# Cluster attention and two MLPs: tokens compared with centroids by small matmuls instead of wide ones and transposes back

## The chip, the core and the metric

The kernel runs on one core of a Trainium2 chip. The metric is the device time of one execution in microseconds. A core has engines that run side by side and wait for each other by semaphores: PE (TensorE) multiplies matrices and writes to PSUM, DVE (VectorE) and ACT (ScalarE) work elementwise and empty PSUM, POOL (GpSimd) works elementwise on SBUF, SP issues DMAs. In the profile PE stands for matmuls and PEld for the loads of their stationary operand.

## What is computed

Attention with a mask made from clusters, then two MLPs (reference, cut to what matters):

```python
q_n = q / (norm(q) + 1e-06); k_n = k / (norm(k) + 1e-06); c_n = centroids / (norm(centroids) + 1e-06)
q_assign = argmax(einsum('bhsd,hcd->bhsc', q_n, c_n), axis=-1)
k_assign = argmax(einsum('bhsd,hcd->bhsc', k_n, c_n), axis=-1)
mask = q_assign[:, :, :, None] == k_assign[:, :, None, :]
scores = where(mask, matmul(q, k.transpose(0, 1, 3, 2)) / sqrt(D), -1e9)
attn = softmax(scores)
x = matmul(attn, v)                       # batch 2, heads 8, tokens 768, width 64; 16 centroids per head
x = (sigmoid(x @ w_gate) * (x @ w_val)) @ w_out
out = relu(x @ w_in2)**2 @ w_out2         # the weights are float64 and are decoded on the chip
```

## The kernel before

All matmuls work on float32 numbers split into a high part of type float32r and a rest (`hi`, `lo`), so that a product takes several matmuls. Two heads of one batch make a pair; there are 8 pairs. Attention runs in 96 units, 12 per pair (2 heads, 2 halves, 3 blocks of 128 queries). In unit n the loop at L926 does, in this order: the maximum of unit n's scores on DVE (L935); what earlier groups left to do on ACT and DVE (`drain`); the transposes on PE of the probabilities of unit n-3 (`evac`, L821) and their copies by ACT (L823) and DVE (L829); the scores of unit n+1 on PE (`scores`, L803); the exponential on ACT (L956); four matmuls with the values of an earlier half (`attend`, L839, L840); and then the steps of the next pair's preparation that a table assigns to this unit. POOL normalises the probabilities (L875).

The preparation of a pair (`prep`) turns q and k (`transposes`, L563; after that hi and lo lie with the head width on the partitions and the tokens along the free dimension), compares the tokens with the 16 centroids of each head, takes the argmax (L656), builds a one-hot row per token (L663 to L679), transposes it (L696) and writes it beside q and k as the mask. The comparison takes four steps per pair: `sims(0)` and `sims(1)` ("s0", "s1") for three blocks of 128 tokens each, and `back(0)` and `back(1)` ("b0", "b1"). `cen` holds the centroids, high and low part, for both heads, with zeros around them.

The tables `STEPS` and, for the second pair, `SECOND_STEPS` say in which unit each step stands, counted from the first unit of the pair that is prepared. The first pair's preparation runs ahead of the loop as a plain list, and between its steps `keep_warm` puts transposes of the identity on PE (L888, the table `WARM`).

What a step computes in PSUM goes into a tile "t" of a pool with three buffers (`ps_t`), which `evac` uses too. Its evacuation (`post`) stands in the next unit's `drain`.

Of the kernel before, what the change touches and what calls it, by code (L numbers as in the profile page):

```python
# [8 lines left out]
F32 = mybir.dt.float32  # L9
# [19 lines left out]
STEPS = {  # L29
    -8: ["tq0"],  # L30
    -7: ["tk0"],
    -6: ["s0"],
    -5: ["tk1"],
    -4: ["tq1"],
    -3: ["b0", "load"],
    -2: ["s1"],
    -1: ["kb", "b1"],
    0: ["qb", "am"],
    1: ["eq"],
    2: ["oh", "on", "ka", "qa"],  # L40
# [5 lines left out]
    -3: ["tk0"],  # L46
    -2: ["tq0"],
    -1: ["tk1"],
    0: ["s0", "tq1"],
    1: ["s1"],  # L50
    2: ["b0", "kb"],
    3: ["b1", "qb"],
    5: ["am"],
    6: ["eq"],
    7: ["oh", "on", "ka", "qa"],
    9: ["mk"],
}

WARM = {-9: 8, -2: 16, -1: 4}


EARLY_PARTS = [3, 3, 9, 10, 15, 18, 19, 21, 27, 30, 30, 33, 34, 39, 42, 43, 45, 51]
# [10 lines left out]
def cluster_attention_two_mlps(  # L73
# [13 lines left out]
    nc = tc.nc  # L87
    B, H, S, D = q.shape
    NCL = centroids.shape[1]
    P = 128  # L90
# [5 lines left out]
    HB = NB // 2  # L96
    NH = HB * P
# [44 lines left out]
    for c in range(CH, F1 // P, CH):  # L142
        a = weights.index(("g", c + CH // 2))
# [175 lines left out]
    with tc.manual_schedule():  # L319
        ident = const.tile([P, P], F32, name="ident")  # L320
# [18 lines left out]
        cen = const.tile([P, 4 * NPAIR + 2, 2 * NCL], F32R, name="cen")  # L339
# [14 lines left out]
        act, parts, banks, split, sgs = {}, {}, {}, {}, {}  # L354
# [99 lines left out]
        with ExitStack() as ac:  # L454
# [3 lines left out]
            am = pc.enter_context(tc.tile_pool(name="am", bufs=1, side="right"))  # L458
# [5 lines left out]
            ps_t = ac.enter_context(tc.tile_pool(name="ps_t", bufs=3, space=PSUM))  # L464
# [83 lines left out]
            def prep(i):  # L548

                b, hp = pairs[i]  # L550
                hi_t, lo_t, keep = {}, {}, {}
# [58 lines left out]
                def sims(n):  # L610


                    def go():
                        sp = ps_t.tile([P, NH], F32, name="t")
                        parts = [(nm, t) for nm in "kq" for t in (hi_t, lo_t)]
                        for x, (nm, t) in enumerate(parts):
                            w = cen[:, 4 * hp + 2 : 4 * hp + 6] if nm == "k" else cen[:, 4 * hp : 4 * hp + 4]
                            nc.tensor.matmul(  # L618
                                sp, w.rearrange("p a c -> p (a c)"), t[nm][:, n * NH : (n + 1) * NH], start=(x == 0), stop=(x == 3)
                            )  # L620

                        def post():
                            keep["sim", n] = am.tile([P, NH], F32, name="sim", bufs=2)
                            nc.scalar.copy(keep["sim", n], sp)

                        return post

                    return go

                def back(n):  # L630
                    def go():
                        bp = ps_t.tile([P, HB, 2, 2, 2 * NCL], F32, name="t")
                        sim = keep.pop(("sim", n))
                        for c in range(HB):
                            nc.tensor.transpose(
                                bp[:, c].rearrange("p a b c -> p (a b c)"), sim[:, c * P : (c + 1) * P], ident
                            )

                        def post():
                            if n == 0:  # L640
                                keep["tot"] = am.tile([P, NB, 2, 2 * NCL], F32, name="tot")
                            o = keep["tot"][:, n * HB : (n + 1) * HB]
                            part = am.tile([P, HB, 2, 2 * NCL], F32, name="part")
                            nc.scalar.copy(part, bp[:, :, :, 1])
                            nc.vector.tensor_tensor(out=o, in0=bp[:, :, :, 0], in1=part, op=ALU.add)

                        return post

                    return go
# [84 lines left out]
                if i == 0:  # L734
                    return [
                        transposes("k", 0),
                        transposes("k", 1),
                        transposes("q", 0),
                        transposes("q", 1),
                        sims(0),  # L740
                        sims(1),
                        stack("k", 0),
                        stack("q", 0),
                        stack("q", 1),
                        back(0),
                        back(1),
                        argmax,
                        equal,
                        stack("k", 1),
                        onehot,  # L750
                        one,
                        first_mask,
                    ]
# [5 lines left out]
                    "load": lambda: load(i + 1, "kq"),  # L759
                    "s0": sims(0),  # L760
                    "s1": sims(1),
                    "b0": back(0),
                    "b1": back(1),
                    "ka": stack("k", 0),
                    "kb": stack("k", 1),
                    "qa": stack("q", 0),
# [137 lines left out]
            for t, f in enumerate(prep0):  # L904
# [9 lines left out]

                keep_warm(WARM.get(t - len(prep0), 0))
            outs, late, st = {}, {}, {}
# [4 lines left out]
            for i in range(1, len(pairs)):  # L921
                for m, group in (prep1 if i == 1 else prep(i)).items():
                    at = (i - 1) * UPP + m
                    todo.setdefault(at, []).append(group)
            st[0] = scores(units[0])
            for n in range(N + LAG + 4):  # L926
                u = units[n] if n < N else None
                w = units[n - LAG] if 0 <= n - LAG < N else None
# [7 lines left out]
                nm = nms.pop(n - 1, None)  # L936
                if nm is not None:
                    p = Pt[units[n - 1]]
# [32 lines left out]
                if w is not None:  # L971
                    Pt.pop(w)
                    if w[3] == HB - 1:
# [3 lines left out]
                        if w[1] == 1:  # L977
                            for t in range(3):
                                at = n + SUMS[w[2]][t] if w[0] < len(pairs) - 1 else n + (3 if end else 6)
# [65 lines left out]
```

## Time and profile before

| | |
|---|---|
| time, median of 3 runs | 820.93 us (820.81 to 821.15) |
| the profiled execution | 821.03 us, its span 819.2 us |
| PE, share of the span with a matmul in it | 98% |
| PEld / DVE / ACT / POOL | 84% / 76% / 54% / 26% |
| start until the first unit's maximum | 0 to 19.8 us |
| attention | to about 266 us |
| the two MLPs | about 266 to 819 us |

The median is over three executions. The profile is of one more, and every duration below is from that one. A busy share counts the time in which at least one instruction of the engine is on record; matmuls overlap in it, so that of PE says little by itself. The chain that ended last is followed back from the last instruction, at each step to what released it.

### The profile page before, as it was taken

What the parts mean: (1) busy time and instruction counts of PE and PEld (TensorE: products, weight loads), DVE (VectorE), ACT (ScalarE), POOL (GpSimd) and SP (SyncE); (2) the same over time, 40 slices, a digit from 0 to 9 for tenths busy, and PEclk for the clock granted to TensorE, in tenths of its full rate; (3) what the DMA queues carried; (4) which work ended last, traced back from release to release, by engine and by line L of the source; (5) the groups of instructions that cost most, each with busy time, mean ns of one, the idle gap of its engine ahead of it and who ended that gap; (6) DMA issues with size and microseconds to landing.
All of it is one profiled execution on the core that took longest, in us unless ns stands there. A gap on an engine that the chain in (4) does not pass through costs nothing.

```text
span 819.2 us, 11691 instructions
## 1 busy us (share of the span) xinstructions
PE 803.1 (98%) x4097; PEld 689.8 (84%) x4097; DVE 625.9 (76%) x1144; ACT 442.1 (54%) x889; POOL 214.2 (26%) x349
## 2 busy tenths in 40 slices
PE   7899999999999999999999999999999999999998
PEld 6789989999998788888888888888888888888886
DVE  5899999999898378657878767769784787788233
ACT  5888889888896223532332223336745733642530
POOL 4668989988884200000000000000000000000000
PEclk9999999999999999999999999999999999999999
DMA  8465455364321122122221212202222212221012
GB/s 190 108 144 144 102 136 121 92 143 96 78 77 44 52 71 95 51 71 68 94 77 52 78 52 78 78 0 89 66 78 77 78 52 77 78 78 52 0 52 102
DMA packets 63274, 67.01 MB, mean 82 GB/s; under 512 B 28624, under 2 KB 54224, under 8 KB 63216
## 3 DMA queue, kind: packets, MB, share of 16 engines
q1 hardware_dynamic: 63216, 66.27, 29.3%
q8 instruction: 32, 0.52, 0.3%
q14 instruction: 26, 0.21, 0.1%
HBM read 45.12 MB, written 3.15 MB: 59 GB/s over the span
## 4 chain that ended last, share of the span: by engine, by line
PE 80%; DVE 12%; POOL 3%; ACT 2%; issue 1%; DMA 1%; SPq 0%; POOLq 0%; ACTq 0%; DVEq 0%
PE bank_b L427 18%; PE bank_a L350 13%; PE bank_a L351 13%; PE bank_a L349 13%; PE bank_a L427 9%; DVE pt_lo L829 4%; PE t L821 4%; DVE nm L935 3%; PE s L803 3%; PE o L839 2%; PE o L840 2%; POOL p L875 1%; PE t L618 1%; PE t L563 1%; PE o L888 1%
## 5 line engine op out<-in xcount | busy, mean ns | idle before, releaser
L350 PE MATMUL bank_a<-x_lo,w 128*128 128x512 f32 x480 | 187.0, 389 | 0.9 <-POOL x_lo L870 0.9
L349 PE MATMUL bank_a<-x_hi,w 128*128 128x512 f32 x480 | 186.9, 389 | 0.0
L351 PE MATMUL bank_a<-x_hi,w 128*128 128x512 f32 x480 | 186.9, 389 | 0.0
L393 DVE TENSOR_TENSOR slo<-act,shi 128x512 fp32r<-128x512 f32 x84 | 57.9, 689 | 66.8 <-ACT shi L392 60.3
L350 PEld LDWEIGHTS bank_a<-x_lo,w 128*128 128x128 f32 x480 | 90.1, 188 | 19.7 <-POOL x_lo L870 1.2
L349 PEld LDWEIGHTS bank_a<-x_hi,w 128*128 128x128 f32 x480 | 90.1, 188 | 18.8 <-POOL x_hi L868 0.2
L351 PEld LDWEIGHTS bank_a<-x_hi,w 128*128 128x128 f32 x480 | 90.1, 188 | 18.8
L829 DVE TENSOR_TENSOR pt_lo<-t,pt_hi 128x384 fp32r<-128x384 f32 x192 | 96.7, 546 | 5.4 <-ACT pt_hi L823 5.4
L875 POOL TENSOR_SCALAR p<-p,nm,ones 128x768 f32<-128x768 f32 x96 | 94.8, 988 | 15.7 <-DVE nm L874 15.3
L956 ACT ACTIVATE p<-s,nm 128x768 f32<-128x768 f32 x96 | 88.0, 917 | 15.9 <-DVE nm L874 10.8
L803 PE MATMUL s<-st_k,st_q 128*128 128x384 f32 (+1 forms) x384 | 91.0, 359 | 0.6 <-ACT p L956 0.5
L935 DVE TENSOR_REDUCE nm<-s 128x1 f32<-128x768 f32 x96 | 91.0, 948 | 0.0
L823 ACT CAST pt_hi<-t 128x384 fp32r<-128x384 f32 x192 | 83.2, 487 | 6.3 <-PE t L821 5.6
L821 PE MATMUL t<-ident,p 128*128 128x128 f32 x576 | 81.6, 275 | 4.3 <-DVE pt_lo L829 3.2
L392 ACT CAST shi<-act 128x512 fp32r<-128x512 f32 x84 | 51.7, 615 | 56.0 <-PE bank_b L427 32.9
L427 PE MATMUL bank_b<-wo,shi 128*128 128x512 f32 x256 | 78.8, 389 | 0.0
L231 ACT CAST w<-wtop 128x512 fp32r<-128x512 f32 x38 | 23.7, 623 | 101.8 <-DVE wtop L249 101.8
L821 PEld LDWEIGHTS t<-ident,p 128*128 128x128 f32 x576 | 66.2, 140 | 11.7 <-issue 4.2
L839 PE MATMUL o<-pt_hi,vt 128*128 128x384 f32 x192 | 65.1, 339 | 0.4 <-ACT oc L845 0.4
L375 DVE TENSOR_TENSOR act<-bank_a,sg 128x512 f32<-128x512 f32 x36 | 24.9, 691 | 53.1 <-PE bank_a L351 50.9
L803 PEld LDWEIGHTS s<-st_k,st_q 128*128 128x128 f32 (+1 forms) x384 | 62.5, 190 | 2.9 <-ACT p L956 2.2
L840 PE MATMUL o<-pt_lo,vt 128*128 128x384 f32 x192 | 64.7, 337 | 0.0
(137 smaller groups left out, 1386.2 us busy)
## 6 DMA issues: line engine op xcount, KB each, us to landing
wraw<-in_moe_w_out_dram SPq DMA_DIRECT2D x28, 512.0 KB, 3.2
wraw<-in_moe_w_in_dram SPq DMA_DIRECT2D x16, 512.0 KB, 3.7
wraw<-in_moe_w_gate_dram SPq DMA_DIRECT2D x11, 512.0 KB, 3.5
wraw<-in_moe_w_val_dram SPq DMA_DIRECT2D x11, 512.0 KB, 3.5
nat_v<-in_v_dram SPq DMA_DIRECT2D x8, 384.0 KB, 3.2
st_k<-st_k SPq DMA_DIRECT2D x16, 192.0 KB, 4.5
x<-oc SPq DMA_DIRECT2D x32, 96.0 KB, 2.1
out_dram<-part SPq DMA_DIRECT2D x12, 256.0 KB, 2.0
```

The lines of the kernel that those rows point to most:

```text
L349: nc.tensor.matmul(bk, w[:, 0, ks], mov_hi[:, kk], start=(kk == 0), stop=False)
L350: nc.tensor.matmul(bk, w[:, 0, ks], mov_lo[:, kk], start=False, stop=False)
L351: nc.tensor.matmul(bk, w[:, 1, ks], mov_hi[:, kk], start=False, stop=(kk == KD - 1))
L427: nc.tensor.matmul(bk, st, mv, start=(first and n == 0), stop=(last and n == 2))
L803: nc.tensor.matmul(st[:, m, :NH], Q[i, e][: DEPTH[e][a], a, c * P : (c + 1) * P], K[i, e][: DEPTH[e][a], a, m * NH : (m + 1) * NH], start= ...
L821: nc.tensor.transpose(tp[:, m, :], Pt[u][:, c * P : (c + 1) * P], ident)
L823: nc.scalar.copy(hi, tp)
L829: nc.vector.tensor_tensor(out=lo, in0=tp, in1=f32(hi), op=ALU.subtract)
L839: nc.tensor.matmul(o, vt, hi[:, c, :], start=(c == 0), stop=False)
L875: nc.gpsimd.tensor_scalar(out=p, in0=p, scalar1=nm[:, 3:4], scalar2=ones, op0=ALU.mult, op1=ALU.mult)
L935: nc.vector.tensor_reduce(out=nms[n][:, 0:1], in_=st[n][:, :, :NH], axis=AX.XY, op=ALU.max, negate=True)
L956: nc.scalar.activation(out=e.rearrange("p (m n) -> p m n", m=2), in_=st.pop(n)[:, :, :NH], func=AF.Exp, bias=nms[n][:, 0:1], accum_out=nms ...
```

## The change

`sims` now takes the tokens as the stationary operand and the centroids as the moving one. For each block of 128 tokens and for k and q there are two matmuls of 64 moved columns, one with the high part of the tokens and one with their low part, each against the high and low part of the centroids of both heads. The result has the tokens on its partitions already, so the copy `sim` by ACT, the three transposes of `back` and that step itself are gone; the copy of `part` and the sum `tot` follow as before, with two buffers for `part`. The steps "s0" and "s1" stand where "b0" and "b1" stood, and eight of the warming transposes ahead of the loop are removed.

```diff
--- before.py
+++ after.py
@@ -29,12 +29,10 @@
 STEPS = {
     -8: ["tq0"],
     -7: ["tk0"],
-    -6: ["s0"],
     -5: ["tk1"],
     -4: ["tq1"],
-    -3: ["b0", "load"],
-    -2: ["s1"],
-    -1: ["kb", "b1"],
+    -3: ["s0", "load"],
+    -1: ["kb", "s1"],
     0: ["qb", "am"],
     1: ["eq"],
     2: ["oh", "on", "ka", "qa"],
@@ -46,17 +44,16 @@
     -3: ["tk0"],
     -2: ["tq0"],
     -1: ["tk1"],
-    0: ["s0", "tq1"],
-    1: ["s1"],
-    2: ["b0", "kb"],
-    3: ["b1", "qb"],
+    0: ["tq1"],
+    2: ["s0", "kb"],
+    3: ["s1", "qb"],
     5: ["am"],
     6: ["eq"],
     7: ["oh", "on", "ka", "qa"],
     9: ["mk"],
 }
 
-WARM = {-9: 8, -2: 16, -1: 4}
+WARM = {-2: 16, -1: 4}
 
 
 EARLY_PARTS = [3, 3, 9, 10, 15, 18, 19, 21, 27, 30, 30, 33, 34, 39, 42, 43, 45, 51]
@@ -611,36 +608,20 @@
 
 
                     def go():
-                        sp = ps_t.tile([P, NH], F32, name="t")
-                        parts = [(nm, t) for nm in "kq" for t in (hi_t, lo_t)]
-                        for x, (nm, t) in enumerate(parts):
-                            w = cen[:, 4 * hp + 2 : 4 * hp + 6] if nm == "k" else cen[:, 4 * hp : 4 * hp + 4]
-                            nc.tensor.matmul(
-                                sp, w.rearrange("p a c -> p (a c)"), t[nm][:, n * NH : (n + 1) * NH], start=(x == 0), stop=(x == 3)
-                            )
-
-                        def post():
-                            keep["sim", n] = am.tile([P, NH], F32, name="sim", bufs=2)
-                            nc.scalar.copy(keep["sim", n], sp)
-
-                        return post
-
-                    return go
-
-                def back(n):
-                    def go():
                         bp = ps_t.tile([P, HB, 2, 2, 2 * NCL], F32, name="t")
-                        sim = keep.pop(("sim", n))
+                        w = cen[:, 4 * hp + 2 : 4 * hp + 4].rearrange("p a c -> p (a c)")
                         for c in range(HB):
-                            nc.tensor.transpose(
-                                bp[:, c].rearrange("p a b c -> p (a b c)"), sim[:, c * P : (c + 1) * P], ident
-                            )
+                            at = slice((n * HB + c) * P, (n * HB + c + 1) * P)
+                            for x, nm in enumerate("kq"):
+                                to = bp[:, c, x].rearrange("p b c -> p (b c)")
+                                nc.tensor.matmul(to, hi_t[nm][:, at], w, start=True, stop=False)
+                                nc.tensor.matmul(to, lo_t[nm][:, at], w, start=False, stop=True)
 
                         def post():
                             if n == 0:
                                 keep["tot"] = am.tile([P, NB, 2, 2 * NCL], F32, name="tot")
                             o = keep["tot"][:, n * HB : (n + 1) * HB]
-                            part = am.tile([P, HB, 2, 2 * NCL], F32, name="part")
+                            part = am.tile([P, HB, 2, 2 * NCL], F32, name="part", bufs=2)
                             nc.scalar.copy(part, bp[:, :, :, 1])
                             nc.vector.tensor_tensor(out=o, in0=bp[:, :, :, 0], in1=part, op=ALU.add)
 
@@ -742,8 +723,6 @@
                         stack("k", 0),
                         stack("q", 0),
                         stack("q", 1),
-                        back(0),
-                        back(1),
                         argmax,
                         equal,
                         stack("k", 1),
@@ -759,8 +738,6 @@
                     "load": lambda: load(i + 1, "kq"),
                     "s0": sims(0),
                     "s1": sims(1),
-                    "b0": back(0),
-                    "b1": back(1),
                     "ka": stack("k", 0),
                     "kb": stack("k", 1),
                     "qa": stack("q", 0),
```

Two places in the order of instructions show it. The first is on PE in units 70 to 72 of the last pair, whose preparation began in unit 64 (its L618 is the wide matmul of `sims`, L635 the transpose of `back`; L821, L803, L839 and L840 are the unit's own work, named above). Before, from the last matmul of unit 70's `attend` on:

```order
L840 MATMUL o<-pt_lo,vt 128x384
L618 MATMUL t<-st_k_143,cen 128x384 x2
L618 MATMUL t<-st_q_145,cen 128x384
L618 MATMUL t<-lo_q,cen 128x384
L821 MATMUL t<-ident,p 128x128 x6
L803 MATMUL s<-st_k_136,st_q_138 128x384 x4
L839 MATMUL o<-pt_hi,vt 128x384
L840 MATMUL o<-pt_lo,vt 128x384
L839 MATMUL o<-pt_hi,vt 128x384
L840 MATMUL o<-pt_lo,vt 128x384
L635 MATMUL t<-ident,sim 128x128 x3
L821 MATMUL t<-ident,p 128x128 x6
```

Now, from the same matmul on (`evac` is L798 here, `scores` L780, `attend` L816 and L817, the small matmuls L617 and L618):

```order
L817 MATMUL o<-pt_lo,vt 128x384
L798 MATMUL t<-ident,p 128x128 x6
L780 MATMUL s<-st_k_136,st_q_138 128x384 x4
L816 MATMUL o<-pt_hi,vt 128x384
L817 MATMUL o<-pt_lo,vt 128x384
L816 MATMUL o<-pt_hi,vt 128x384
L817 MATMUL o<-pt_lo,vt 128x384
L617 MATMUL t<-cen,st_k_143 128x64
L618 MATMUL t<-cen,st_k_143 128x64
L617 MATMUL t<-cen,st_q_145 128x64
L618 MATMUL t<-cen,lo_q 128x64
```

Eight more rows like the last four follow now, and then the six transposes of unit 72. The wide group of unit 70 is gone, as is the one of unit 66, and twelve small matmuls stand where three transposes stood at the end of unit 71; so it is in unit 69.

The second is on ACT ahead of the loop, in the preparation of the first pair (`cen` are the centroids, st_q_138 the high part of q, sim and part the copies that were named). Before:

```order
L539 CAST cen<-t 64x4x16 x2
L568 ACTIVATE st_q_138<-t 128x384 x2
L624 COPY sim<-t 128x384 x2
L644 COPY part<-t 128x192 x2
L568 ACTIVATE st_k_143<-t 128x384
L568 ACTIVATE st_q_145<-t 128x384
```

Now:

```order
L536 CAST cen<-t 64x4x16 x2
L565 ACTIVATE st_q_138<-t 128x384 x2
L625 COPY part<-t 128x192 x2
L565 ACTIVATE st_k_143<-t 128x384
L565 ACTIVATE st_q_145<-t 128x384
```

The two copies `sim` are gone, so that `part` follows the evacuation of q directly. DVE, POOL and SP keep their instructions; the sum `tot` stands one unit behind "s0" and "s1", as it stood behind "b0" and "b1".

## Rows read from the trace of the kernel before

**Rows 1.** The page: busy time of each engine, share of the span, instructions.
```profile
...
PE 803.1 (98%) x4097; PEld 689.8 (84%) x4097; DVE 625.9 (76%) x1144; ACT 442.1 (54%) x889; POOL 214.2 (26%) x349
...
```

**Rows 2.** Windows: from, to, length, busy time (instructions) by engine, granted clock, DMA.
```profile
...
20.00:41.00 21.00, 18.40 (x113) 15.19 (x112) 18.92 (x40) 17.21 (x40) 14.08 (x22) 1.00 0.50 114
...
180.00:210.00 30.00, 29.61 (x205) 28.46 (x206) 28.05 (x60) 26.61 (x64) 25.69 (x40) 1.00 0.43 95
...
266.00:819.20 553.20, 548.39 (x2417) 453.05 (x2415) 384.20 (x640) 220.41 (x380) 5.77 (x8) 1.00 0.20 67
...
```

**Rows 3.** Chain that ended last, 181 to 210 us: start, length (us), what.
```profile
...
187.21 0.69 PE t L618 x4
...
194.72 0.33 PE t L635 x3
...
197.10 0.71 PE t L618 x4
...
197.83 0.48 ACT sim L624
...
200.29 0.33 ACT part L644
...
200.64 0.04 DVE tot L645
...
207.33 0.56 DVE oh L679
...
209.43 0.70 PE t L821 x4
```

**Rows 4.** Timeline of PE, 196 to 212 us: start, length (us), what.
```profile
...
199.71 0.49 PE L635 MATMUL t<-ident,sim 128*128 128x128 f32 x3
...
206.23 0.82 PE L821 MATMUL t<-ident,p 128*128 128x128 f32 x6
207.01 0.97 PE L803 MATMUL s<-st_k,st_q 128*128 128x384 f32 x4
...
208.61 0.52 PE L696 MATMUL t<-identb,oh 128*64 128x128 bf16 x6
209.43 0.92 PE L821 MATMUL t<-ident,p 128*128 128x128 f32 x6 [0.30 <-DVE pt_lo L829]
...
```

**Rows 5.** Line L618: duration in ns, shortest/median/longest, first and last start.
```profile
...
L618 PEld LDWEIGHTS t<-x_hi,cen x6: 187/188/189, 9.7 to 108.1; 128*128 128x128 f32 x6
L618 PE MATMUL t<-x_hi,cen x6: 336/338/444, 9.7 to 108.3; 128*128 128x384 f32 x6
...
```

**Rows 6.** Line L635, the same columns.
```profile
...
L635 PEld LDWEIGHTS t<-ident,sim x48: 137/141/144, 11.5 to 199.8; 128*128 128x128 f32 x48
L635 PE MATMUL t<-ident,sim x48: 270/272/332, 11.6 to 199.9; 128*128 128x128 f32 x48
...
```

**Rows 7.** Groups of instructions by form: busy us, mean ns, idle before.
```profile
...
L803 PEld LDWEIGHTS s<-st_k,st_q 128*128 128x128 f32 x288 | 45.7, 190 | 2.9 <-ACT p L956 2.2
...
```

**Rows 8.** Timeline of all engines, 8.9 to 14 us.
```profile
...
9.75 0.19 PEld L618 LDWEIGHTS t<-x_hi,cen 128*128 128x128 f32 x1 [0.31 <-DVE x_hi L569]
...
9.86 0.37 PEld L618 LDWEIGHTS t<-st_k,cen 128*128 128x128 f32 x2
...
10.23 0.48 ACT L624 COPY sim<-t 128x384 f32<-128x384 f32 x1 [0.74 <-PE t L618]
...
10.73 1.03 PE L888 MATMUL o<-ident 128*128 128x128 f32 x8
...
11.60 0.82 PE L635 MATMUL t<-ident,sim 128*128 128x128 f32 x6
12.13 0.32 ACT L644 COPY part<-t 128x192 f32<-128x192 f32 x1 [0.72 <-PE t L635]
...
12.92 0.32 ACT L644 COPY part<-t 128x192 f32<-128x192 f32 x1 [0.48 <-DVE tot L645]
...
13.67 0.55 DVE L656 TENSOR_REDUCE mx<-tot 128x24 f32<-128x384 f32 x1
...
```

## Prediction

> **What bounds the kernel now.** The page comes first: PE has work in 98% of the span [rows 1]. That share alone proves little, because a matmul's record lasts longer than the spacing in a stream: six transposes of line L635 stand in 0.82 us, so they start 0.11 us apart, while one of them is recorded for 0.27 us [rows 6, 8]. So I went on by stages. The windows show three of them [rows 2]. From 266 us on the two MLPs run, PE busy in 548 of 553 us; nothing there changes, and a shift at its start reaches the end in full. From 20 to 41 us PE has work in 18.4 of 21 us only, and DVE in 18.9: the first pair of heads is not bound by PE. From 180 to 210 us, which holds the preparation of the last pair (units 64 to 75), PE has 29.6 of 30 us, DVE 28.1 and ACT 26.6: three nearly full engines, so the chain must say whose time counts. It runs on PE alone from 181 to 197.8 us, through both groups of wide matmuls (L618, 0.69 and 0.71 us) and the first group of transposes back (L635, 0.33 us). Then it passes through ACT (the copy of sim, 0.48 us) to the copy of part at 200.29 and DVE's sum at 200.64 us, stays on DVE through the argmax and the one-hot, and returns to PE at 209.43 us [rows 3]. So in every pair about 17 us go at PE's pace and about 12 at that of ACT and DVE, and the comparison stands at the end of PE's part.
>
> **What is removed.** Per pair, on PE: two groups of four wide matmuls at 0.70 us and two groups of three transposes at 0.33 us [rows 3], together 2.06 us. On ACT: two copies of sim at 0.48 us [rows 3, 8]. In the first pair also eight warming transposes (L888), which filled PE while the copies ran [rows 8]; small matmuls stand there now, so their removal is put at nothing.
>
> **What is added.** Per pair 24 small matmuls, each with its own load of 128 stationary columns and 64 columns moved. The trace has no such matmul, so the price c of one is bounded. Its load can be seen bare once: at 9.75 us PE had waited for x_hi, and the following load began at 9.86 us, 0.11 us later [rows 8]. The record of the matmul says the same: 444 ns where the load was exposed against a median of 338 ns, so 106 ns [rows 5]. For the f32 transposes the same difference is 332 - 272 = 60 ns [rows 6]. The fp32r loads are recorded at 187 to 190 ns, those of line L803 too, which hold tokens as the new ones will, and the transposes' loads at 141 [rows 5 to 7]; the 48 ns between them fit the 46 ns between 106 and 60. The wide matmuls run 0.70 / 4 = 0.175 us apart although each has such a load, so the load is hidden behind the matmul ahead. 384 columns at the granted 1.00 (the 2.4 GHz level) [rows 2] are 0.160 us, so 0.015 us of that spacing is something else. A small matmul is too short to hide a load of 0.108 us: 64 columns are 0.03 us. c lies between 0.108 (loads back to back) and 0.123 us (that plus the 0.015); I take 0.112, near the bare loads. 24 x 0.112 = 2.69 us against 2.06: PE gets 0.63 us more per pair (0.53 to 0.89).
>
> The Trainium skill speaks for a lower price: its page "TensorE: Matmul & The Clock Gate", section "Back-to-back issue gap", gives about 81 ns per matmul for a stream of load and matmul pairs with 128 columns moved. The transposes here move 128 columns and stand 109 ns apart, so this trace doesn't reach that figure. By it 24 would take 1.94 us, 0.12 less than now.
>
> **Where it lies.** In units counted from a pair's first, the work stood at -6 (wide), -3 (back), -2 (wide) and -1 (back). Now twelve small ones (1.34 us) stand at -3 and twelve at -1. All four places but the last lie in the stretch that the chain follows on PE, so their balance counts in full. At -1 the new group stands, as the transposes back did, behind the unit's other PE work, and what is queued behind it are the transposes of p of the next unit and their copies on ACT and DVE, which waited in the same order before. The hand-over gains a little: the transposes back end at 199.71 + 0.49 = 200.20 us [rows 4], and ACT came to part at 200.29 us [rows 3], held up by the copy of sim. Without it part starts at the end of the matmuls: 0.09 us back. Net 0.54 us per pair. The other copy is off the path, and part and the sum on DVE keep their size, so ACT's freed 0.96 us counts for no more.
>
> Six pairs (units 4 to 75) are prepared in this stage: 6 x 0.54 = **+3.2 us** (2.7 to 4.8 over the bounds of c).
>
> **The start.** For pair 0 everything waits for the argmax at 13.67 us [rows 8]. The chain there was: wide matmuls, copy of sim (10.23), transposes back (11.60), copy of part (12.13, then 12.92, since its one buffer had to be read first), sum, argmax. In the changed kernel three of the 24 small matmuls are through when x_hi arrives at 9.75 us; 21 follow at 0.112 us, so the last starts at about 12.1 us. Its result takes about 0.2 us, and from the start of the copy of part to the argmax it is 13.67 - 12.92 = 0.75 us [rows 8]: the argmax comes at 13.05 us, **-0.6 us** (-0.4 at c = 0.123). The second part no longer waits, having a second buffer.
>
> **The second pair** (units 0 to 3, in the stage from 20 to 41 us) had its wide matmuls in units 0 and 1, where PE waits, and the transposes in 2 and 3; now twelve small ones stand in each of 2 and 3, a little over 1 us more in each. PE's gaps there (2.6 us in 21 [rows 2]) are the cover. Bounds: nothing, and one pair's full 0.63 us; I take **+0.2**.
>
> **Sum.** The profiled execution took 821.03 us (span 819.2), 0.10 us above the median of the runs, 820.93. 821.03 + 3.2 - 0.6 + 0.2 = **823.8 us**. Its own range, with all terms at their bounds, is 821.03 + 2.7 - 0.6 + 0 = 823.1 to 821.03 + 4.8 - 0.4 + 0.63 = 826.1; a PE that runs out of work in a unit that lost its wide matmuls, or finds more, widens that to 822.3 to 826.5.
>
> **Rivals.**
> *Absorbed.* Behind DVE's stretch PE waits before it goes on: at 206.23 us six transposes take 0.78 us where 6 x 0.109 = 0.65 would do, and the masks' transposes at 208.61 us need about 0.35 until the next start, which comes at 209.43 [rows 4]: some 0.6 us per pair in all. If the delay fell into these gaps, only the start's gain would stay: 821.03 - 0.6 = 820.4 us, no change. Against it: the gaps are made by DVE's work, which begins only when the comparison ends, so they move with it.
> *Cheap loads (the other side).* If a load of tokens in a stream cost what a transpose's load does, 0.060 us [rows 6], then c would be about 0.06: 24 x 0.06 = 1.44 us, 0.62 less per pair than now, with the hand-over 0.71. Six pairs give -4.3, the start -1.1 more than above (21 x 0.052), so 821.03 - 4.3 - 1.7 = 815.0 us. It decides at c = 0.086, where 24 c is 2.06. Against it stand all fp32r loads, at 187 to 190 ns [rows 5, 7]. The 81 ns of the Trainium skill's page, cited above, lie on this side of that point; by them it would be 6 x -0.21 and -0.6 - 0.65 at the start, 818.5 us.
> *No overlap.* If a load couldn't run behind so short a matmul, or a narrow fp32r matmul streamed at a slower pace, c would be the load plus the matmul: 0.108 + 64 columns at the pace of the f32 transposes (0.109 / 2 = 0.055) = 0.163, at worst 0.108 + 0.109 = 0.217 us. Per pair that is +1.85 - 0.09 to +3.15 - 0.09, over six pairs +10.6 to +18.4, the start +0.5 to +1.6, the second pair 0.2 to 1: 832 to 842 us, 835 as a value. For it speaks only that no narrow fp32r matmul stands in the trace; against it, that wide ones hide their loads.
> The same page of the Trainium skill, section "The mechanism" under the packing of small matmuls, says that loads overlap matmuls in flight only when the row groups differ, which would be this case; the 0.175 us of the wide ones, which use the whole array, disagree.
>
> **Chances.** PE pays: 0.68. Absorbed: 0.14. Cheap loads: 0.09. No overlap: 0.09. The bound of a measurable change is 0.2%, 1.6 us. Of the first case a small part (0.03) falls below it. Slower: 0.65 + 0.09 = 0.74; same: 0.14 + 0.03 = 0.17; faster: 0.09. The range takes in the absorbed case and the likeliest one's bounds with room above for a price between it and no overlap: 820.0 to 828.5 us; the last two cases, 0.18, stay outside.
>
> **What the profile after would show.** Spacing of the small matmuls: 0.11 us (my price), 0.06 (cheap) or 0.16 and more (no overlap). Each group of twelve on the chain with about 1.35 us in the pairs from 41 us on, and part right behind it. Argmax of pair 0 at 13.05 us. Periods of the last pairs longer by 0.5 us, and the first MLP's start later by some 2.8 us. I am wrong if these pairs keep their period though c is 0.11 (absorbed), or if PE turns out to wait for DVE or ACT in the units that lost the wide matmuls, so that the removed 1.40 us there aren't gained: the loss would then be up to twice as large.

## The result and the profile after

| | before | changed |
|---|---|---|
| median, us | 820.93 | 824.99 |
| executions, us | 820.15 to 821.90 (19) | 822.39 to 827.82 (19) |
| profiled execution, us (span) | 821.03 (819.2) | 822.53 (820.7) |

The ratio of changed to before is 1.0056, with a 95% interval of [1.0043, 1.0068]: slower. The forecast was 823.8 us, slower. The executions of the changed kernel lie in three groups, four at 822.4 to 823.1 us (mean granted clock 0.998), seven at 824.5 to 825.1 (0.995 or 0.996) and eight at 827.3 to 827.8 (0.989 to 0.994), while the kernel before, where its clock is on record (beside the experiments), kept 0.997 to 1.0. The first profile is of the first group.

The page of the changed kernel, engines' row (as [rows 1]), then the windows (as [rows 2]; the last one is taken 1.5 us later, since the span is that much longer):

```profile
...
PE 806.2 (98%) x4169; PEld 695.2 (85%) x4169; DVE 625.5 (76%) x1144; ACT 437.7 (53%) x873; POOL 214.4 (26%) x349
...
```

```profile
...
20.00:41.00 21.00, 18.00 (x120) 15.41 (x120) 19.01 (x41) 16.77 (x39) 14.91 (x23) 1.00 0.50 120
180.00:210.00 30.00, 29.69 (x212) 28.64 (x211) 27.48 (x59) 25.45 (x59) 25.06 (x40) 1.00 0.42 94
267.50:820.70 553.20, 548.71 (x2418) 453.33 (x2417) 384.06 (x640) 220.49 (x380) 5.87 (x8) 1.00 0.21 67
...
```

PE has 72 matmuls more and 3.1 us more work. The MLPs take their 548 us as before. In the stretch of the last pair PE is as full as it was.

The place where the small matmuls stand in that pair, in the chain that ended last (start, length, what), and in PE's timeline (L798 is `evac`, L816 and L817 `attend`):

```profile
...
200.54 0.17 PE o L817
200.72 0.03 PE t L617
200.75 0.11 PE t L618
200.86 0.11 PE t L617
...
201.87 0.11 PE t L618
201.98 0.39 PE t L798 x3
...
202.45 0.49 ACT pt_hi L800
```

```profile
...
200.56 0.19 PE L617 MATMUL t<-cen,st_k 128*128 128x64 f32 x1
200.59 0.28 PE L618 MATMUL t<-cen,st_k 128*128 128x64 f32 x1
...
201.70 0.28 PE L618 MATMUL t<-cen,lo_q 128*128 128x64 f32 x1
201.81 0.87 PE L798 MATMUL t<-ident,p 128*128 128x128 f32 x6
...
```

All twelve stand on the chain. From the second (200.59) to the twelfth (201.70) there are ten spacings in 1.11 us: 0.111 us each, against the 0.112 that was forecast. Their loads are recorded as long as all fp32r loads (line L617; shortest/median/longest in ns):

```profile
...
L617 PEld LDWEIGHTS t<-cen,st_q x48: 190/192/272, 8.6 to 201.6; 128*128 128x128 f32 x48
L617 PE MATMUL t<-cen,st_q x48: 277/277/379, 8.7 to 201.6; 128*128 128x64 f32 x48
...
```

The start, all engines, 9 to 14 us (as [rows 8]):

```profile
...
9.19 0.30 PE L618 MATMUL t<-cen,x_hi 128*128 128x64 f32 x1 [0.26 <-DVE x_hi L566]
...
10.42 0.32 ACT L625 COPY part<-t 128x192 f32<-128x192 f32 x1 [1.49 <-PE t L618]
...
11.33 0.38 PE L617 MATMUL t<-cen,st_q 128*128 128x64 f32 x1
...
11.53 0.40 PE L618 MATMUL t<-cen,x_hi 128*128 128x64 f32 x1
...
11.96 0.32 ACT L625 COPY part<-t 128x192 f32<-128x192 f32 x1 [1.22 <-PE t L618]
...
12.71 0.55 DVE L637 TENSOR_REDUCE mx<-tot 128x24 f32<-128x384 f32 x1
...
```

The argmax comes at 12.71 us instead of 13.67. The last two matmuls stand 0.2 us apart: the granted clock was at half there (the 1.2 GHz level) from 11.4 to 14.8 us, where before it was at 1.00 throughout. In the row of that stretch, as in all rows of windows, the clock is the figure behind POOL's:

```profile
...
11.40:14.70 3.30, 3.30 (x17) 3.30 (x17) 2.21 (x4) 1.30 (x3) 1.01 (x2) 0.50 0.58 120
...
```

Where the time went is best read from the starts of units. In the timeline of DVE each unit has one reduction nm of 768 columns (L935 before, L912 now); its start marks the unit. The steps of a pair's preparation are counted, in the code, from the first unit of the pair ahead of it, so units 4 to 15 hold the preparation of the third pair and units 64 to 75 that of the last. "Again a" and "again b" are two more profiles of the changed kernel, explained below. Four of the rows that the table is read from, unit 4 in the changed kernel and in again a, and unit 76 before and in the changed kernel:

```profile
...
27.01 0.95 DVE L912 TENSOR_REDUCE nm<-s 128x1 f32<-128x768 f32 x1
...
28.36 0.95 DVE L912 TENSOR_REDUCE nm<-s 128x1 f32<-128x768 f32 x1
...
209.66 0.95 DVE L935 TENSOR_REDUCE nm<-s 128x1 f32<-128x768 f32 x1
...
211.56 0.95 DVE L912 TENSOR_REDUCE nm<-s 128x1 f32<-128x768 f32 x1
...
```

| unit starts, us | before | changed | again a | again b |
|---|---|---|---|---|
| 0 | 19.80 | 18.95 | 19.08 | 18.91 |
| 4 | 27.88 | 27.01 | 28.36 | 28.71 |
| 16 | 60.36 | 60.41 | 64.68 | 65.42 |
| 28 | 90.69 | 90.52 | 94.81 | 95.55 |
| 40 | 121.50 | 121.47 | 125.76 | 126.52 |
| 52 | 150.96 | 151.59 | 155.89 | 156.65 |
| 64 | 180.32 | 181.57 | 185.88 | 186.63 |
| 76 | 209.66 | 211.56 | 215.85 | 216.61 |
| whole execution | 821.03 | 822.53 | 826.78 | 827.59 |

The three profiles of the changed kernel need the same time from unit 16 to 76: 151.15, 151.17 and 151.19 us. What they differ by is complete at unit 16.

### The profile page after: what moved, and what is told of

The parts are those of the page before. It is cut to its first block, busy times and chain, and to the rows that moved or that the text cites. A ratio compares the mean times of both kernels' runs of the same rounds, so it can differ in the third digit from the quotient of the medians.

```text
span 820.7 us, 11817 instructions
## 1 busy us (share of the span) xinstructions
PE 806.2 (98%) x4169; PEld 695.2 (85%) x4169; DVE 625.5 (76%) x1144; ACT 437.7 (53%) x873; POOL 214.4 (26%) x349
## 4 chain that ended last, share of the span: by engine, by line
PE 81%; DVE 11%; POOL 2%; ACT 2%; DMA 1%; issue 1%; SPq 0%; ACTq 0%; DVEq 0%; POOLq 0%
PE bank_b L424 18%; PE bank_a L347 13%; PE bank_a L348 13%; PE bank_a L346 13%; PE bank_a L424 9%; PE t L798 4%; PE s L780 4%; DVE pt_lo L806 4%; DVE nm L912 3%; PE o L816 2%; PE o L817 2%; PE t L618 1%; PE t L617 1%; POOL p L852 1%; ACT pt_hi L800 1%
## 5 line engine op out<-in xcount | busy, mean ns | idle before, releaser
L347 PEld LDWEIGHTS bank_a<-x_lo,w 128*128 128x128 f32 x480 | 90.1, 188 | 19.6 <-POOL x_lo L847 1.0
L780 PE MATMUL s<-st_k,st_q 128*128 128x384 f32 (+1 forms) x384 | 90.9, 359 | 1.8 <-ACT p L933 1.6
L912 DVE TENSOR_REDUCE nm<-s 128x1 f32<-128x768 f32 x96 | 90.8, 946 | 0.0
L798 PE MATMUL t<-ident,p 128*128 128x128 f32 x576 | 81.9, 277 | 3.3 <-DVE pt_lo L806 3.0
L798 PEld LDWEIGHTS t<-ident,p 128*128 128x128 f32 x576 | 65.4, 140 | 10.8 <-issue 3.9
L780 PEld LDWEIGHTS s<-st_k,st_q 128*128 128x128 f32 (+1 forms) x384 | 62.5, 190 | 4.0 <-ACT p L933 4.0
L816 PE MATMUL o<-pt_hi,vt 128*128 128x384 f32 x192 | 65.0, 339 | 0.4 <-ACT oc L822 0.4
L817 PE MATMUL o<-pt_lo,vt 128*128 128x384 f32 x192 | 64.7, 337 | 0.0
```

What stands on the lines that cost most here:

```text
L347: nc.tensor.matmul(bk, w[:, 0, ks], mov_lo[:, kk], start=False, stop=False)
L780: nc.tensor.matmul(st[:, m, :NH], Q[i, e][: DEPTH[e][a], a, c * P : (c + 1) * P], K[i, e][: DEPTH[e][a], a, m * NH : (m + 1) * NH], start= ...
L798: nc.tensor.transpose(tp[:, m, :], Pt[u][:, c * P : (c + 1) * P], ident)
L816: nc.tensor.matmul(o, vt, hi[:, c, :], start=(c == 0), stop=False)
L912: nc.vector.tensor_reduce(out=nms[n][:, 0:1], in_=st[n][:, :, :NH], axis=AX.XY, op=ALU.max, negate=True)
```

## The experiments

Two questions were open: is the price per small matmul (0.111 us, paid in full on the chain) the cause, and what are the 2 to 5 us that most executions have on top? Each kernel was timed beside the kernel before on the same chip (medians 821.28, 820.73 and 821.19 us in the three timed groups, each on another chip).

**The warming transposes put back.**

```
-WARM = {-2: 16, -1: 4}
+WARM = {-7: 8, -2: 16, -1: 4}
```

> The changed kernel with the eight warming transposes put back ahead of the loop, behind the small matmuls of the first pair. Theory A (the price of the small matmuls alone makes the difference; what lies above 822.5 us in the changed kernel's executions comes from a clock that falls in the first pair's preparation, where these transposes are missing): granted clock back to 1.00, times within 1 us of each other, median 822.4 to 823.3 us. Theory B (the clock falls behind groups of small matmuls anywhere in attention, whatever stands ahead of the loop): clock again 0.99 to 0.998 from execution to execution, times spread over 822 to 828 us, median about 825.

Measured: 825.68 us (824.22 to 830.11), ratio 1.0062 [1.0044, 1.0079]. No execution came back to 822.5 and the clock was 0.987 to 0.998, so theory A, that their absence makes the clock fall, is not borne out. In the profile unit 0 came 0.6 us later than in the first of the changed kernel; 0.28 of it is the arrival of x_hi (9.47 against 9.19 us), and the clock fell in both. Nothing here speaks against putting their removal at nothing, but the run doesn't price it.

**The first pair as before, the others small**; **only the first pair small.** Both forms of the comparison stand in one kernel and the pair i chooses (the first table of steps likewise; part has one buffer, as before):

```
...
-                    "s0": sims(0),
-                    "s1": sims(1),
+                    "s0": sims(0) if i > 0 else wide(0),
+                    "s1": sims(1) if i > 0 else wide(1),
+                    "b0": back(0),
+                    "b1": back(1),
...
```

For the second kernel the condition is i == 0.

> The first pair compared as before (wide matmuls, copies, transposes back, eight warming transposes), all others by small matmuls; one buffer for part. Price of the pairs in the loop alone: 820.9 + 2.8 = 823.7 us. Theory A (the clock falls only in the first pair's preparation): clock 1.00 in every execution, spread under 1 us, 823.7. Theory B (it falls in the loop): spread of several us as in the changed kernel, median 825 to 827.

> The reverse: only the first pair compared by small matmuls and without the eight warming transposes, all others as before; one buffer for part. The start alone should give 820.9 - 0.85 = 820.1 us. Theory A: the clock falls in some executions, times spread up to 825 us. Theory B: at most one half-clock stretch ahead of the loop, all executions at 820 to 820.5 us. If the gain of the start does not reach the end, 820.9.

Measured: with the first pair wide 826.06 us (823.05 to 828.19), ratio 1.0055 [1.0038, 1.0071]; only the first pair small 822.40 us (819.56 to 823.65), 1.0011 [1.0001, 1.0020]. Most of the loss sits behind the first pair. In the first kernel the two executions at a clock of 1.0 took 823.05 and 823.59 us, three at 0.996 took 825.9 to 826.2. Its profile (826.22 us) has half the clock from 23.4 to 30.2 us, and units 3 and 4 take 4.64 and 3.42 us there; in the first profile of the changed kernel, at full clock, they take 2.82 and 2.26. That is 3.0 us. When its clock fell no small matmul had run at all: the first one stands at 24.38 us in its timeline of PE.

The second kernel should have gained 0.85 us and lost 1.1 in the median, at clocks of 0.995 to 0.998: small matmuls in the first pair lose clock too. Its profile (822.40 us) has unit 0 at 21.07 us, 2.1 later than the changed kernel's first profile, behind a stretch at half the clock. The first row is of the first kernel, the second of the second:

```profile
...
23.40:30.20 6.80, 6.80 (x31) 6.80 (x30) 3.71 (x9) 3.62 (x8) 4.86 (x8) 0.50 0.73 149
...
10.30:17.00 6.70, 6.70 (x34) 6.70 (x34) 2.69 (x6) 1.62 (x4) 2.54 (x4) 0.50 0.44 111
...
```

**Every small matmul of the loop's pairs twice** (the second set writes the same values over the first):

```
-                            for x, nm in enumerate("kq"):
+                            for x, nm in enumerate("kq" * (2 if i > 0 else 1)):
+                                x %= 2
```

> The changed kernel with every small matmul of the pairs in the loop issued twice (the second time over the first's result, so that the output is the same): 24 more per pair. If PE's time counts in full in the six pairs from 41 us on: 6 x 24 x 0.1115 = 16.1 us more, and 0 to 2.7 for the second pair, so 839 to 844 us. If gaps behind the argmax absorb PE work: under 12 us more, below 837. If the clock falls behind small groups (theory B), it should fall more often here and the time lie above 844 in some executions.

Measured: 845.38 us (843.24 to 848.60), ratio 1.0300 [1.0281, 1.0318]. The units 52 to 63 and 64 to 75 take 32.66 us each instead of 29.98 and 29.99: 2.67 us for 24 more, 0.111 us each; the three pairs from unit 16 on take 2.72 to 2.74 more each. Nothing of it is absorbed. Three of the four executions lie above the 844 us that the price allowed, as was expected if the clock falls more often behind small groups; in the profile, the slowest of them, it is 0.69 from 8 to 41 us:

```profile
...
8.00:41.00 33.00, 30.77 (x167) 29.12 (x166) 19.41 (x38) 15.32 (x34) 13.29 (x22) 0.69 0.57 126
...
```

**128 columns instead of 64 moved by each** (zeros stand beside the centroids):

```
...
-                            for x, nm in enumerate("kq"):
-                                to = bp[:, c, x].rearrange("p b c -> p (b c)")
+                            to = bp[:, c].rearrange("p a b c -> p (a b c)")
+                            for nm, a in (("k", 2), ("q", 0)):
+                                w = cen[:, 4 * hp + a : 4 * hp + a + 4].rearrange("p a c -> p (a c)")
...
```

> The changed kernel with 128 moved columns in every small matmul instead of 64: the centroids with the zeros beside them, k's and q's matmuls of a block of tokens accumulating into the same 128 columns. As many matmuls and loads as in the changed kernel. Theory L (the load of the tokens sets the price of a small matmul): spacing unchanged at 0.11 us. Theory S (the moved columns have a share in it): 0.14 to 0.22 us, 24 of them per pair, so 4 to 16 us more. On the clock: if it falls because the small groups give PE too little to do ahead of 41 us, it stays at 1.00 here more often, and the executions lie at 822 to 823.5 us; if the loads themselves or the missing transposes are the cause, they spread over 822 to 828 us as before.

Measured: 825.38 us (822.49 to 827.41), ratio 1.0057 [1.0039, 1.0076]. In its timeline of PE the second to the twelfth of the last group stand at

```profile
...
203.51 0.28 PE L618 MATMUL t<-cen,st_k 128*128 128x128 f32 x1
...
204.63 0.28 PE L618 MATMUL t<-cen,lo_q 128*128 128x128 f32 x1
...
```

1.12 us for ten spacings, and the last pair takes 30.00 us instead of 29.99. The columns cost nothing. That the load sets the spacing, and not a fixed cost of every pair of load and matmul, was not tried by an edit. But the spacing is that of the bare load, and a pair with another load runs faster: the masks' six transposes in bf16 at 208.61 us [rows 4], whose loads hold 64 columns, take 0.52 us, of which one's record is 0.22, so they stand 0.06 us apart with 128 columns moved.

**The first two pairs as before, six small** (the same edit, i > 1).

> The first two pairs compared as before (wide matmuls, transposes back, warming transposes), pairs 2 to 7 by small matmuls; one buffer for part. The small groups stand only where PE has no gaps. Theory B1 (the clock falls only where small groups stand in a stage in which PE waits, ahead of 41 us): granted clock as in the kernel before, spread under 1.5 us, and the price of six pairs alone, 2.8 us, on top of it: 823.7 to 824.2 us. If the clock falls behind small groups everywhere: spread up to 828 us.

Measured: 823.10 us (822.18 to 824.20), ratio 1.0029 [1.0018, 1.0041], clock 0.997 to 1.0 in all six executions. So the six later pairs alone cost 2.4 us (in its profile units 4 to 75 take 184.21 us, 2.43 more than before), and the executions at 825 to 828 us are gone with the change in the first two pairs. Its profiled execution, the slowest (824.20), has one fall of the clock all the same, from 17.7 to 21.1 us, where no small matmul had run yet. The kernel before varies in the same way, if less: its executions beside this one took 819.62 us (clock 1.0) to 822.33 (0.997).

**Only the first pair small, with 128 columns.**

> Only the first pair by small matmuls, with 128 moved columns each, all others as before; one buffer for part. If the clock holds: the start's gain of 0.9 us reaches the end, 820.0 to 820.4 us in every execution, faster than both kernels. If the clock falls as in the run with only the first pair small: median 822.4.

Measured: 821.07 us (819.36 to 822.45, 11 executions), ratio 1.0003 [0.9993, 1.0012]: no difference to before. Five executions at 0.999 or 1.0 took 819.4 to 820.2 us, the six others, at 0.995 to 0.998, 821.1 to 822.5. The kernel before took 819.6 to 821.3 us beside it at 0.999 or 1.0. It is the best version found that computes the whole, and no better than the kernel before.

**Half the small matmuls in the loop's pairs.** The low parts of the tokens are left out of the comparison there, so part of the computation is missing.

```
-                                nc.tensor.matmul(to, hi_t[nm][:, at], w, start=True, stop=False)
-                                nc.tensor.matmul(to, lo_t[nm][:, at], w, start=False, stop=True)
+                                nc.tensor.matmul(to, hi_t[nm][:, at], w, start=True, stop=(i > 0))
+                                if i == 0:
+                                    nc.tensor.matmul(to, lo_t[nm][:, at], w, start=False, stop=True)
```

> The changed kernel without the matmuls of the tokens' low parts in the pairs in the loop: twelve small matmuls per pair instead of 24 (part of the computation is left out). If PE's time counts in full in both directions: 12 x 0.1115 = 1.34 us less per pair, 0.72 below the kernel before in each of the six pairs from 41 us on; the fastest executions at 822.5 - 8.0 = 814.5 us, 0 to 1.3 less for the second pair. If another engine takes over as the bound when PE has less to do: not below 818 us.

Measured: 820.55 us (818.13 to 822.55, clock 0.989 to 0.998), ratio 1.0001 [0.9990, 1.0012]. In the sum the second case holds, not below 818 us; in the last two pairs the first does. Twelve fewer at 0.1115 us are 1.34 us per pair. The last two pairs give back 1.37 and 1.36, but those of units 16 to 51 give 0.66 at most and one of them takes 0.5 more. So not every pair is bound by PE in both directions. The trace of the kernel before shows it: its chain from 90.5 to 121.5 us (units 28 to 39) is led by DVE's lines, with PE's matmuls far behind:

```profile
...
by line: DVE pt_lo L829 28.3%; DVE nm L935 27.9%; DMA st_k<-row 6.2%; issue 6.0%; DVE spare L246 4.2%; DVE st_k L569 3.0%; ACT row L700 2.8%; DVE nm L874 2.7%; PE t L821 2.6%; SPq L691 2.6%; DVE spare L249 2.5%; DVE spare L242 2.4%; DVE eq 
...
```

**The changed kernel again**, unaltered, two executions, for profiles of its slower executions.

> The changed kernel once more, for a profile of one of its slower executions (most of its runs took 824.4 to 827.8 us, while its first profile shows one of 822.5). Theory: what such an execution has over 822.5 us lies ahead of 41 us. Then a stretch at half the granted clock stands between 20 and 41 us, unit 4 starts later than at 27.01 us by most of the difference, and from unit 16 to unit 76 the units take 151.15 us as in the first profile, within 0.3 us. Rival: the excess is spread over the stages behind (the pairs from 41 us on, or the MLPs); then unit 4 stands at 27.0 us and the distances behind it grow. If this execution takes 822.4 to 823.1 us it tells nothing new.

> The same kernel, a second execution, with the same expectations: at 824.5 us or more a half clock between 20 and 41 us and unit 4 later than at 27.01 us by most of the excess over 822.5 us (theory), or unit 4 at 27.0 us and longer distances behind it (rival).

Measured: 826.78 and 827.59 us, 4.25 and 5.06 us above the first profile; at unit 16 the starts are later by 4.27 and 5.01 us (table above). The whole excess arises ahead of that unit. One part of the expectation failed: unit 4 comes only 1.35 and 1.70 us later, so most of the excess arises between units 4 and 16. The windows of a show the clock, and PE's timeline what it does:

```profile
...
20.00:23.40 3.40, 1.95 (x11) 1.62 (x11) 2.94 (x6) 2.62 (x6) 2.12 (x5) 1.00 1.07 258
23.40:33.60 10.20, 10.20 (x47) 10.10 (x47) 5.54 (x13) 5.58 (x13) 5.15 (x9) 0.50 0.43 102
33.60:41.00 7.40, 7.01 (x47) 5.96 (x46) 7.29 (x16) 5.81 (x13) 4.67 (x8) 1.00 0.01 2
...
```

```profile
...
23.26 0.27 PE L618 MATMUL t<-cen,st_k 128*128 128x64 f32 x1
23.36 0.37 PE L617 MATMUL t<-cen,st_q 128*128 128x64 f32 x1
23.55 0.40 PE L618 MATMUL t<-cen,x_lo 128*128 128x64 f32 x1
23.76 0.40 PE L617 MATMUL t<-cen,st_k 128*128 128x64 f32 x1
...
```

Early in the group of unit 2 the matmuls go from 0.11 to 0.21 us apart, and PE, which had waited for 1.45 of 3.4 us, has no gap left for ten. In b the half clock lasts from 22.6 to 36.3 us, and a first stretch lies ahead of unit 0, from 12.4 to 15.8. The rival (the excess spread over later stages) is wrong.

In b the second pair's first small matmul starts only when the clock has fallen:

```profile
...
22.60:36.30 13.70, 13.70 (x60) 13.60 (x59) 7.91 (x18) 7.54 (x17) 7.09 (x12) 0.50 0.37 82
...
23.40 0.26 PE L617 MATMUL t<-cen,st_k 128*128 128x64 f32 x1
...
```

So that pair's small matmuls can't have set off this fall, nor any small matmul the one at 23.4 us in the kernel with the first pair wide. What stands ahead of both is units 0 and 1 without their wide matmuls.

**The second pair's groups in units 0 and 1.** The kernel before had wide matmuls there (`SECOND_STEPS`), the changed one none of the comparison. From 19.6 to 23.0 us PE had 2.86 us of work before, 1.76 in the first profile of the changed kernel and 1.78 in a. That could be what lets the clock fall, whatever the shape of the matmuls. The rows, before and in the changed kernel:

```profile
...
19.60:23.00 3.40, 2.86 (x18) 2.59 (x16) 2.91 (x5) 2.77 (x7) 0.99 (x3) 1.00 0.85 226
...
19.60:23.00 3.40, 1.76 (x9) 1.36 (x9) 3.19 (x6) 2.37 (x6) 1.85 (x5) 1.00 1.08 268
...
```

```
-    0: ["tq1"],
-    2: ["s0", "kb"],
-    3: ["s1", "qb"],
+    0: ["s0", "tq1"],
+    1: ["s1"],
+    2: ["kb"],
+    3: ["qb"],
```

> The changed kernel with the second pair's two groups of twelve small matmuls in units 0 and 1, where the wide ones of the kernel before stood, in place of units 2 and 3; nothing else differs. Theory (the place): the clock falls because PE had only 1.8 us of work in the 3.4 us from 19.6 to 23.0 us, against 2.9 us before, since the wide matmuls left units 0 and 1. With the small ones there PE has 2.7 us or more in that stretch, the granted clock stays at 1.0 between 20 and 41 us, unit 4 comes at 27.0 us or earlier, and most executions take 822.0 to 823.1 us; median about 822.5. Rival (the small matmuls themselves): a stream of matmuls of 64 columns lets the clock fall wherever it stands. Then half clock still shows between 20 and 41 us, unit 4 comes after 28 us, and the median stays at 824.5 to 826 us.

A second kernel has the same table and 128 columns in every small matmul.

> The same, and each small matmul moves 128 columns (the centroids with zeros beside them) in every pair. By the theory of the place: as with 64 columns, median about 822.5, and ahead of 20 us the clock holds too in most executions, so that the least of them come near 821.5 to 822. By the theory of the small matmuls alone, with twice the columns the fall becomes rarer, but as the variant with 128 columns in units 2 and 3 took 825.4 us, this one stays at 824 or more.

Measured: with 64 columns 824.99 us (822.65, 822.89, 824.99, 825.25, 825.88), ratio 1.0043 [1.0030, 1.0056]; with 128 columns 822.97 us, ratio 1.0029 [1.0017, 1.0042], six of eight executions at 822.8 to 823.1 with a clock of 0.998 to 1.0, the others at 824.8 and 827.2. The place alone keeps the time at 822.4 to 823.1 us in two of five, against four of 19 for the changed kernel; the columns alone did in one of six; both together in six of eight. Neither theory stands by itself, the counts are small, and of these kernels only the two with the early groups ran on the same chip. In the profile with 64 columns (822.65 us) PE has 3.38 us of work from 19.6 to 23.0 and the clock is 1.00 from 20 to 41 us; none of the three slower ones was profiled. The profile of the 827.15 us shows a fall that began earlier still, at 18.2 us, behind a stretch in which PE had 1.69 us of work in 3.4; ahead of the fall in the kernel with two wide pairs it had 1.56. The first row of each pair below is the stretch ahead of the fall, the second what followed; the first pair is of the kernel with two wide pairs, the second of that with early groups of 128 columns:

```profile
...
14.20:17.60 3.40, 1.56 (x16) 1.22 (x15) 3.19 (x7) 0.07 (x1) 0.51 (x1) 1.00 1.02 233
17.70:21.00 3.30, 3.20 (x15) 3.00 (x14) 2.26 (x4) 2.54 (x5) 0.00 (x0) 0.50 0.95 251
...
```

```profile
...
14.70:18.10 3.40, 1.69 (x15) 1.43 (x16) 3.26 (x7) 1.44 (x3) 0.00 (x0) 1.00 1.05 227
18.20:31.80 13.60, 13.60 (x57) 13.41 (x56) 8.44 (x16) 7.35 (x17) 6.20 (x11) 0.50 0.74 164
...
```

## Why the prediction was right, and where it was not

**The price c: right.** 0.112 was forecast and 0.111 us measured, at 64 and at 128 columns. The load is not hidden, and by its bare time it sets the pace. That settles *cheap loads* and *no overlap*, which needed 0.06 and 0.163. The 81 ns of the Trainium skill's page "TensorE: Matmul & The Clock Gate" (section "Back-to-back issue gap") are for 128 columns moved; the variant with 128 columns is that case, and the trace has 0.111 us. The rule in the Trainium skill's section "The mechanism" on the same page, that loads overlap matmuls in flight only when the row groups differ, does not hold here either: matmuls of the whole array follow each other at about the bare load's 0.106 to 0.11 us [rows 5, 8], with no room for the streaming beside it. An earlier sentence of that section of the Trainium skill also lets a load run ahead when it targets the background weight buffer; no run here shows which buffer a load went to.

**Paid in full: right for the last pairs, the hand-over gain wrong.** Forecast were 0.63 us more on PE and 0.09 back at the hand-over, 0.54 net. The pairs of units 40 to 75 take 0.66, 0.62 and 0.65 us more (from the table: 30.12 - 29.46, 29.98 - 29.36, 29.99 - 29.34). 24 x 0.1115 - 2.06 = 0.62 accounts for all of it; nothing came back. Behind the group the chain of the changed kernel runs on through the next unit's transposes of p to DVE (201.98 us in the rows above), and part is no longer on it, although the prediction expected it right behind the group. *Absorbed* is wrong there, as the doubled matmuls show most directly.

**Six equal pairs: wrong in the distribution, close in the sum.** The prediction read one pair's chain and multiplied by six. The first three of the six pairs moved by +0.92, -0.22 and +0.14 us; DVE leads the chain in at least one of them. This is no accident of one profile: units 4 to 15 take 32.5 us in all three profiles with wide matmuls there and 33.0 to 33.4 in the five with the whole set of small ones at full clock. The six together came to +2.77 us (184.55 - 181.78) against +3.2, and to +2.4 in the kernel where only they are small. Why the first of them pays more than its matmuls cost was not tried.

**The start: right.** From x_hi's arrival to the argmax 3.92 us passed before (9.75 to 13.67) and 3.30 were forecast. The two further profiles have 3.31 (9.71 to 13.02, 9.53 to 12.84). The first has 3.52 (9.19 to 12.71), because its clock fell for the last two matmuls; that x_hi came 0.56 us earlier there made up for it. It arrives between 9.19 and 9.91 us over the profiles of all kernels.

**The second pair: +0.2 forecast, none at full clock.** Units 0 to 3 take 8.06 us instead of 8.08. PE's gaps covered the groups, at the lower of the bounds.

**The sum.** The forecast of +2.8 us over the profiled 821.03 was made for a clock that stays up, and is to be held against the first profile, which has +1.5: -0.85 at unit 0, nothing in the second pair, +2.77 in six pairs make +1.90 at unit 76, and the stages behind took 0.4 less (610.97 us against 611.37). The profiles of the variants, which change nothing there, lie between 610.8 and 611.9.

**What was not foreseen.** The median lies 1.2 us above the forecast and 2.5 above that first profile, since 15 of 19 executions take 2 to 5 us more at a lower mean clock. Where that was profiled (again a and b), the clock falls to the 1.2 GHz level ahead of 41 us; no execution at 824.5 to 825.1 us was profiled. The prediction took the granted 1.00 of [rows 2] as given. Its step on the second pair, "PE's gaps there are the cover", holds at full clock only. At the half clock PE has no gaps, and a group of twelve takes 2.6 us (12 x 0.213) instead of 1.3. With the first two pairs wide the executions at 825 us and more are gone, while with only the first pair wide, and with only the first pair small, two to three us are lost in most executions. So the changes in both pairs ahead of unit 4 cost clock. That the forecast came within 1.2 us of the median is thus partly luck: pairs a little cheaper than reckoned, and a clock that the prediction had not reckoned with.

## What to carry to other kernels

When wide matmuls are replaced by narrow ones whose stationary operand changes each time, count loads, not columns: measure the bare load in the trace and multiply (here 64 and 128 columns cost the same behind an fp32r load). Before one pair's chain is multiplied by the number of pairs, read the chain of each, since the bound engine can differ. And where work is taken away from a stretch in which TensorE already waits, look at the granted clock as something that the change can lose, in several executions and not in one profile.

## What the chip showed unexpectedly

- A kernel can have several times with nothing but the granted clock between them: 822.5, 824.8 and 827.5 us for the same program. In the three executions that were profiled the whole difference is made ahead of unit 16, by 3 to 17 us at the half clock.
- 64 or 128 columns moved cost the same 0.111 us behind an fp32r load; with 128 columns the clock held more often (five of 11 executions at 0.999 or 1.0 with only the first pair small, none of 11 with 64). These two ran on different chips, on which the kernel before had 0.999 or 1.0 in 17 of 24 and in 8 of 17 executions. But the profiles agree: with 64 columns in the first pair seven of eight show a fall between 9.8 and 12.6 us, with 128 columns none of three, with wide matmuls none of three.
- What exactly lets the clock fall stays open. Ahead of the falls at 17.7, 18.2 and 23.4 us PE waited for a good part of the time, but in the first profile it waited as much (1.76 us of work from 19.6 to 23.0) without a fall behind it; and the fall at 11.4 us came when PE had been at work nearly all the time, with small matmuls (2.88 us from 8.0 to 11.3). The small matmuls can't be the whole of it, since two falls came before any had run (17.7 and 23.4 us in the kernels with the first pairs wide). A version that fills the units ahead with wide work was not tried.
